# Chunked attention and a mixture of experts on one core: q and k loaded eight tokens to a partition, K read at strides

## The chip, the core and the metric

The kernel runs on one core of a Trainium2 chip. The core has five engines with instruction streams of their own: TensorE (PE in the profile, its weight loads PEld), VectorE (DVE), ScalarE (ACT), GpSimd (POOL) and SyncE (SP). PE multiplies matrices from the on-chip memory SBUF and writes the result to a second one, PSUM, from which DVE and ACT fetch it. DMA queues move data between the device's memory and SBUF. The metric is the device time of one execution in microseconds (us).

## The reference

```python
# attention: q, k, v are (4 batches, 8 heads, 768 tokens, 64)
chunk, left_ctx, right_ctx = (32, 16, 8)
for c in range(768 // 32):
    c_start, c_end = 32 * c, 32 * c + 32
    l_start, r_end = max(0, c_start - 16), min(768, c_end + 8)
    k_full = concatenate([mem_k, k[:, :, l_start:r_end]], axis=2)   # 8 + up to 56 keys
    v_full = concatenate([mem_v, v[:, :, l_start:r_end]], axis=2)
    a = softmax(q[:, :, c_start:c_end] @ k_full.T / 8)
    out[:, :, c_start:c_end] = a @ v_full
x = out.transpose(0, 2, 1, 3).reshape(3072, 512)      # tokens x all heads
# mixture of experts
y_dense = relu(x @ w1_dense) @ w2_dense
expert = argmax(x @ w_gate, axis=1)                   # one of 8 experts
gate = softmax(x @ w_gate)[token, expert]
y = y_dense + gate * (relu(x @ w1[expert]) @ w2[expert])
```

All arrays are float32; the result has 3072 rows of 512.

## The kernel before

**Attention** goes over 16 pairs, each of two heads of one batch. The 128 partitions hold the two heads' 64 dimensions beside each other. The order of all instructions is written out by hand for every engine's queue, and each engine takes its own in that order.

`load_qk` (line 258) brings q and k of a pair from the device's memory with a cast to bf16, each into a tile in which a partition holds `U = 6` consecutive tokens of both heads: partition p holds tokens 6p to 6p + 5. POOL issues these loads, q's and k's four pairs ahead. `transpose_qk` (line 357) then turns them on PE: for each of the six places u and each head one transpose, 64 columns of weights by 128 moving columns, into a PSUM bank `tp`. The bank holds the tokens sorted by u first: column u * 128 + p is token 6p + u. The copies out of the bank put the tokens back in order, reading the bank at strides:

```python
srcv = tp[:, :S].rearrange("d (u p) -> d p u", u=U)
nc.scalar.copy(dT.rearrange("d (p u) -> d p u", u=U), srcv)      # q, line 374
lo = nc.vector.tensor_copy(dst[:D, 0], srcv[:D])                 # k, first head, line 378
hi = nc.scalar.copy(dst[D:, 1], srcv[D:])                        # k, second head, line 379
```

k's copy goes to one of two tiles `kbd`, where each head has its own 64 partitions and its own half of the columns, with zeros elsewhere, so that one matmul gives both heads' scores.

`scores` (line 384) multiplies q with the memory keys (6 matmuls, line 388) and, for each of the 24 chunks, 32 query columns as weights with up to 56 key columns of both heads, 112 moving columns (line 401). The four chunks of a tile go to four column groups of PE. Then come `maximum` (DVE, line 411), `softmax` (subtraction on DVE, line 417, and the exponential on ACT, line 422), `probs_back` (PE transposes the probabilities, line 428, and ACT copies them out, line 430), `values` (line 438, in two halves of 12 chunks), and `scaled` (DVE, a reciprocal at line 449 and a product at line 450). `gate_part` and `gate_sum` work out the gate's logits: transposes at line 470, copies on ACT at line 473, matmuls at line 495, sums on DVE at lines 506 and 508. `record` casts the pair's result to bf16 into a row buffer (ACT, line 480) and puts each row's token number beside it (lines 485 and 487), from a small table `tok`: row p of tile t is token 128 t + p. `tok` is made once by an iota on POOL and cast to float by DVE in `constants_cast` (line 761) in the third pair.

In turn i of the main loop (line 794) the engines get, in this order: the scores of pair i + 1, `scaled` of pair i - 1, the probabilities' transposes of pair i, the maximum and softmax of pair i + 1, the first half of the values of pair i, `transpose_qk` of pair i + 2, the second half of the values, and `record` and `gate_sum` of pair i - 1. On DVE the copy of k thus stands between the softmax of pair i + 1 and `scaled` of pair i. On ACT the exponential, the copy of q and the copy of k follow one another.

**Routing.** When a batch is done, `choose`, `ranks` and `rank` find each token's expert and its row among that expert's rows (PE and DVE), and `rows_out` (line 585) scatters the rows into `x_reg` in the device's memory (POOL, line 589). Every row carries its gate and its token number.

**Experts.** `x_reg` is fetched in tiles of 128 rows (SP), transposed (line 204), multiplied with the dense weights (lines 218 and 234) and with the tile's expert's weights (lines 218 and 955), and the rows are scattered to the output by their token numbers (POOL, line 964).

Of the kernel before, what the change touches and what calls it, by code (L numbers as in the profile page):

```python
# [11 lines left out]
F32 = mybir.dt.float32  # L12
BF16 = mybir.dt.bfloat16
AF = mybir.ActivationFunctionType
ALU = mybir.AluOpType
AX = mybir.AxisListType
I32 = mybir.dt.int32
# [3 lines left out]
def kernel(  # L21
# [14 lines left out]
    nc = tc.nc  # L36

    B, H, S, D = q.shape
# [6 lines left out]
    KEYS = n_mem + CTX  # L45
# [2 lines left out]
    NP = H // 2  # L48
    T = S // 128
    CPT = 128 // CHUNK  # L50
    U = 6
    PU = S // U
    PE_, DVE_ = mybir.EngineType.PE, mybir.EngineType.DVE
    ACT_, POOL_, SP_ = (
# [23 lines left out]
    r_pool = ctx.enter_context(tc.tile_pool(name="r_pool", bufs=1))  # L78
# [22 lines left out]
    def bank():  # L101
        return ps2.tile([128, 512], F32, tag="tp", name="tp")

    identity = singles.tile([128, 128], BF16, name="identity")
# [15 lines left out]
    to_cast = []  # L120
# [124 lines left out]
    st_ = [dict() for _ in range(NPAIR)]  # L245
# [7 lines left out]
    NK = 2  # L253
    kbd = [a_const.tile([128, 2, S], BF16, name=f"kbd{i}") for i in range(NK)]
# [3 lines left out]
    def load_qk(pi, names="qk"):  # L258

        b, hp = divmod(pi, NP)  # L260
        for nm, src in (("q", q), ("k", k)):
            if nm not in names:
                continue
            t_ = a_load.tile([PU, 2, U * D], BF16, tag=f"{nm}_bf", name=f"{nm}_bf")
            nc.gpsimd.dma_start(
                t_, src[b, 2 * hp:2 * hp + 2].rearrange("h (p u) d -> p h (u d)", u=U)
            )
# [89 lines left out]
    def transpose_qk(pi):  # L357

        for nm in ("q", "k"):
            bf = st_[pi].pop(nm + "b")  # L360
            tp = bank().bitcast(BF16)
            for u in range(U):
                for hh in range(2):
                    r0 = hh * D
                    nc.tensor.transpose(  # L365
                        tp[r0:r0 + D, u * PU:(u + 1) * PU],
                        bf[:, hh, u * D:(u + 1) * D],
                        identity,
                        tile_position=(0, r0),
                    )  # L370
            srcv = tp[:, :S].rearrange("d (u p) -> d p u", u=U)
            if nm == "q":
                dT = a_work.tile([128, S], BF16, tag="qT", name="qT")
                nc.scalar.copy(dT.rearrange("d (p u) -> d p u", u=U), srcv)
                st_[pi]["qT"] = dT
            else:
                dst = kbd[pi % NK].rearrange("d h (p u) -> d h p u", u=U)
                lo = nc.vector.tensor_copy(dst[:D, 0], srcv[:D])  # L378
                hi = nc.scalar.copy(dst[D:, 1], srcv[D:])  # L379
                tc.declare_no_dep(  # L380
                    hi.ins, lo.ins, reason="the two heads have partitions of their own"
                )

    def scores(pi):
        qT, kb = st_[pi].pop("qT"), kbd[pi % NK]
        for t in range(T):
            o = (t % TB) * 2 * KEYS
            nc.tensor.matmul(
                sc[:, t // TB, o:o + 2 * KEYS].rearrange(
                    "p (h k) -> p h k", k=KEYS)[:, :, CTX:],  # L390
                qT[:, t * 128:(t + 1) * 128],
                mkT[:, pi],
            )
        for t in range(T):
            o = (t % TB) * 2 * KEYS
            for cc in range(CPT):
                c = t * CPT + cc
                l = max(0, c * CHUNK - LEFT)
                r = min(S, c * CHUNK + CHUNK + RIGHT)
                k0 = l - (c * CHUNK - LEFT)  # L400
                nc.tensor.matmul(  # L401
                    sc[cc * CHUNK:(cc + 1) * CHUNK, t // TB, o:o + 2 * KEYS].rearrange(
                        "p (h k) -> p h k", k=KEYS)[:, :, k0:k0 + r - l],
                    qT[:, c * CHUNK:(c + 1) * CHUNK],
                    kb[:, :, l:r],
                    tile_position=(0, cc * CHUNK),
                )

# [337 lines left out]
    def constants():  # L746
        nc.gpsimd.affine_select(
            upper, ones, pattern=[[1, 128]], compare_op=ALU.is_ge, fill=0.0,
            base=-1, channel_multiplier=-1,
        )  # L750
        slot_no = iota_f32(NB, "slot_no")
        slot128 = iota_f32(NB, "slot128", step=128)
        desc = iota_f32(E, "desc", base=E, step=-1)
        pcol = iota_f32(1, "pcol", step=0, cm=1)
        tok = iota_f32(T, "tok", step=128, cm=1)
        base_a = iota_f32(NA, "base_a", base=128, step=128)
        reg25 = iota_f32(E, "reg25", base=1, step=ROWS // 128)
        reg0 = iota_f32(E, "reg0", base=128, step=ROWS)
        return slot_no, slot128, desc, pcol, tok, base_a, reg25, reg0

    def constants_cast():
        for tf, ti in to_cast:
            nc.vector.tensor_copy(tf, ti)
        nc.vector.tensor_copy(seen_bf, reg25)

    transpose_qk(0)
    scores(0)
    maximum(0)
    softmax(0)
# [24 lines left out]
    for i in range(NPAIR):  # L794
# [69 lines left out]
        if i == 1:  # L864
            slot_no, slot128, desc, pcol, tok, base_a, reg25, reg0 = constants()
# [108 lines left out]
    while w_todo:  # L974
        src, dst = w_todo.pop(0)
# [82 lines left out]
```

## Time and profile before

| | |
|---|---|
| time, median of 3 runs | 240.48 us (240.46 to 241.56) |
| the profiled execution | 243.27 us |
| its span, first to last instruction | 241.5 us |
| mean granted TensorE clock | 0.966 |
| instructions | 7851 |
| PE busy | 198.7 us |
| DVE busy | 157.4 us |
| ACT busy | 135.5 us |
| POOL busy | 144.8 us |

The profile is of one execution. Its busy times say how long an engine had an instruction under way; how long a stage takes is decided by what its instructions wait for. In the rows that follow, `<-` after the busy time names what an engine was idle for. `x24` is a count of instructions; where a row merges several, its time runs from the first start to the last end.

### The profile page before, as it was taken

The page shows a single profiled execution, that of the slowest core. Times are in us where ns is not written, and L with a number is a line of the kernel's source. Part 1 is how long each engine was busy: PE and PEld are TensorE (multiplying, and loading weights), DVE is VectorE, ACT ScalarE, POOL GpSimd, SP SyncE. Part 2 cuts the span into 40 slices and gives each one's busy share as a digit, 9 for nine tenths or more (in the row PEclk, how much of TensorE's full clock was granted, in tenths as well). Part 3 has the DMA queues.
Part 4 walks back from the last instruction along what each step waited for, and adds up shares of the span by engine and source line. Part 5 has one row for each costly group of instructions (what it writes and reads, how often), then busy time and mean ns, then how long its engine had stood idle before and what let it go on. Part 6 is the DMA issues. An engine that isn't in the chain of part 4 may idle for free.

```text
span 241.5 us, 7851 instructions
## 1 busy us (share of the span) xinstructions
PE 198.7 (82%) x3147; PEld 148.4 (61%) x3147; DVE 157.4 (65%) x372; ACT 135.5 (56%) x205; POOL 144.8 (60%) x215
## 2 busy tenths in 40 slices
PE   1687597989788978887738999999999999999960
PEld 0466475766656656665517777777777866766630
DVE  4688969789878879878714661322224678788750
ACT  7257666896879777987322455555556622222210
POOL 7976983606997499958401871121222068888881
PEclk9999979999999999999795999999999999999997
DMA  5999999998999999999998549999999323433432
GB/s 89 195 178 159 131 164 182 167 155 152 147 177 188 161 146 178 200 167 250 192 174 166 104 101 184 264 189 201 184 148 174 62 90 155 182 129 123 164 138 83
DMA packets 59879, 38.57 MB, mean 160 GB/s; under 512 B 35646, under 2 KB 57534, under 8 KB 59840
## 3 DMA queue, kind: packets, MB, share of 16 engines
q0 software_dynamic: 21584, 25.20, 59.6%
q1 hardware_dynamic: 37216, 11.77, 29.1%
q10 hardware_dynamic: 1040, 1.06, 1.8%
q8 instruction: 27, 0.44, 0.8%
q14 instruction: 12, 0.10, 0.2%
HBM read 43.22 MB, written 11.30 MB: 226 GB/s over the span
## 4 chain that ended last, share of the span: by engine, by line
POOL 23%; DMA 20%; issue 10%; PE 6%; DVE 5%; ACT 2%; POOLq 1%; ACTq 0%; DVEq 0%
DMA w_all<-in_moe_w_dram 16%; POOL out_dram L964 12%; POOL x_reg L589 5%; POOL idle L583 4%; DMA x_reg<-rec,row_i 3%; PE sc L218 2%; PE av L438 1%; DVE x L450 1%; DMA xg<-x_reg 1%; PE tp L365 1%; DVE dif L417 1%; DVE mx L411 1%; ACT kbd L379 1%; PE tp L470 1%; POOLq L964 0%
## 5 line engine op out<-in xcount | busy, mean ns | idle before, releaser
L589 POOL DMA_INDIRECT x_reg<-rec,row_i x24 | 26.8, 1118 | 23.3 <-ACT rec L480 14.4
L964 POOL DMA_INDIRECT out_dram<-y,dst_i x27 | 29.0, 1074 | 14.3 <-DVE y L960 10.6
L438 PE MATMUL av<-vw,at 128*32 128x130 f32 x768 | 31.0, 296 | 7.0 <-issue 3.9
L438 PEld LDWEIGHTS av<-vw,at 128*32 128x32 f32 x768 | 22.1, 116 | 14.2 <-issue 8.7
L224 ACT ACTIVATE h<-sc 128x512 bf16<-128x512 f32 x27 | 16.1, 597 | 24.3 <-PE sc L218 24.3
L353 POOL COPY vw<-vw 24x1536 f32<-24x1536 f32 x15 | 23.2, 1545 | 10.6 <-DMA vw<-in_v_dram 6.5
L218 PEld LDWEIGHTS <-w_st 128*128 128x128 bf16 x432 | 25.5, 98 | 5.8 <-DVE w_st L942 3.2
L218 PEld LDWEIGHTS <-w1d 128*128 128x128 bf16 x432 | 27.0, 101 | 2.3 <-issue 1.8
L942 DVE COPY w_st<-w_all 128x2048 bf16 x27 | 19.8, 738 | 5.6 <-PE sc L218 4.1
L224 ACT ACTIVATE xT_B<-sc 128x512 bf16<-128x512 f32 x16 | 9.6, 597 | 23.4 <-PE sc L218 23.4
L378 DVE COPY kbd<-tp 64x768 bf16<-64x768 bf16 x16 | 15.2, 948 | 11.0 <-PE tp L365 11.0
L207 DVE COPY xT_B<-tp 128x512 bf16<-128x512 bf16 x16 | 6.8, 424 | 23.4 <-PE tp L204 23.3
L422 ACT ACTIVATE a<-dif 128x768 f32<-128x768 f32 x16 | 13.5, 844 | 13.9 <-DVE dif L417 12.2
L234 PE MATMUL av<-w2d,h 128*128 128x512 bf16 x72 | 19.2, 390 | 0.0
L977 POOL CAST scratch<-w_all 1x1 f32<-1x1 bf16 x10 | 1.7, 174 | 28.9 <-DMA w_all<-in_moe_w_dram 28.9
L473 ACT COPY xT<-tp 128x384 f32<-128x384 f32 x32 | 14.0, 489 | 6.8 <-PE tp L470 6.8
L470 PE MATMUL tp<-identity_f,x 128*128 128x128 f32 x96 | 13.6, 276 | 4.9 <-DVE x L450 2.4
L430 ACT COPY at<-at_ps 128x768 f32<-128x768 f32 x16 | 12.8, 798 | 7.8 <-PE at_ps L428 7.6
L218 PE MATMUL sc<-xT_B,w_st 128*128 128x128 bf16 x256 | 16.9, 219 | 0.2 <-DVE w_st L942 0.2
L218 PE MATMUL sc<-xT_B,w1d 128*128 128x128 bf16 x256 | 16.9, 219 | 0.0
L411 DVE TENSOR_REDUCE mx<-sc 128x12 f32<-128x768 f32 x16 | 15.3, 956 | 1.7 <-PE sc L401 1.3
L417 DVE TENSOR_TENSOR dif<-sc,mx 128x768 f32<-128x768 f32 x16 | 15.3, 958 | 1.6
(160 smaller groups left out, 449.2 us busy)
## 6 DMA issues: line engine op xcount, KB each, us to landing
w_all<-in_moe_w_dram POOLq DMA_DIRECT2D x14, 512.0 KB, 6.9
vw<-in_v_dram SPq DMA_DIRECT2D x30, 200.0 KB
xg<-x_reg SPq DMA_DIRECT2D x27, 129.0 KB
q_bf<-in_q_dram POOLq DMA_DIRECT2D x16, 192.0 KB, 7.7
k_bf<-in_k_dram POOLq DMA_DIRECT2D x16, 192.0 KB, 7.2
vw<-in_mem_v_dram SPq DMA_DIRECT2D x32, 48.0 KB
x_reg<-fill ACTq DMA_DIRECT2D x1, 1032.0 KB
w_all<-in_moe_w_dram POOLq DMA_DIRECT2D x4, 256.0 KB, 8.5
```

The costliest lines, as they stand in the source:

```text
L218: written(place, nc.tensor.matmul(ph[:, f, :], w[:, d, f * 128:(f + 1) * 128], xT[:, d, :], start=(d == 0), stop=(d == DT - 1),))
L224: was_read(place, nc.scalar.activation(h_sb, ph, AF.Relu))
L234: written(place, nc.tensor.matmul(pd, h_d[:, f, :], w2d_sb[:, f, :], start=(f == 0), stop=(f == FT - 1)))
L353: copy(vt[p0 + CHUNK:p0 + CTX, :NCH, hh, :D], vt[p0:p0 + n, 1:, hh, :D])
L378: lo = nc.vector.tensor_copy(dst[:D, 0], srcv[:D])
L411: nc.vector.reduce_max(mx, scv, axis=AX.X)
L417: nc.vector.tensor_tensor(dif.rearrange("p (b t) (h k) -> p b (t h) k", b=2, h=2), scv, mx.to_broadcast([128, 2, T, KEYS]), ALU.subtract,)
L438: nc.tensor.matmul(av[cc * CHUNK:(cc + 1) * CHUNK, t // TB, (t % TB) * W2:(t % TB + 1) * W2], at[:, t, cc * CHUNK:(cc + 1) * CHUNK], vt[:, ...
L470: nc.tensor.transpose(xtt[:, t * 128:(t + 1) * 128], xb[:, t0 + t, :], identity_f32)
L589: inst = nc.gpsimd.indirect_dma_start(x_reg, bass.IndirectOffsetOnAxis(ap=row_i[:, t:t + 1], axis=0), rec[:, t, :], None,)
L942: nc.vector.tensor_copy(w_st[:, None], w1_all[:, bass.ds(e_dve.pop(s), 1), :, :])
L964: inst = nc.gpsimd.indirect_dma_start(out, bass.IndirectOffsetOnAxis(ap=dst_i[:, s:s + 1], axis=0), y, None, bounds_check=N_tokens - 1, oo ...
```

## The change

q and k are loaded with eight tokens to a partition, on 96 partitions in place of 128. Each has 16 transposes of 96 moving columns in place of 12 of 128.

For k the bank keeps the order that the transposes give, sorted by u first, and so does `kbd`: both copies read and write runs. `scores` picks the keys of a chunk, which begin and end at multiples of eight tokens, out of `kbd` with an access pattern of a step of 96 elements over u, and its result has the keys in token order.

For q the transposes write to the bank at steps: in every group of 16 columns, the two tokens that two neighbouring partitions hold at place u lie side by side, so column 16 g + 2 u + s holds token 16 g + 8 s + u. The copy reads and writes runs, and the queries stay in that order, in which every group of 16 is complete. So the rows of the attention's result are permuted within groups of 16, and the table of token numbers is changed to match by six small DVE instructions, once.

```diff
-    U = 6
+    U = 8
     PU = S // U
...
             tp = bank().bitcast(BF16)
+            pairs = tp[:, :S].rearrange("d (g u s) -> d u g s", u=U, s=2)
+            plain = tp[:, :S].rearrange("d (u g s) -> d u g s", u=U, s=2)
+            to = pairs if nm == "q" else plain
             for u in range(U):
                 for hh in range(2):
                     r0 = hh * D
                     nc.tensor.transpose(
-                        tp[r0:r0 + D, u * PU:(u + 1) * PU],
+                        to[r0:r0 + D, u],
                         bf[:, hh, u * D:(u + 1) * D],
-                        identity,
+                        identity[:PU, :PU],
                         tile_position=(0, r0),
                     )
-            srcv = tp[:, :S].rearrange("d (u p) -> d p u", u=U)
             if nm == "q":
                 dT = a_work.tile([128, S], BF16, tag="qT", name="qT")
-                nc.scalar.copy(dT.rearrange("d (p u) -> d p u", u=U), srcv)
+                nc.scalar.copy(dT, tp[:, :S])
                 st_[pi]["qT"] = dT
             else:
-                dst = kbd[pi % NK].rearrange("d h (p u) -> d h p u", u=U)
-                lo = nc.vector.tensor_copy(dst[:D, 0], srcv[:D])
-                hi = nc.scalar.copy(dst[D:, 1], srcv[D:])
+                dst = kbd[pi % NK]
+                lo = nc.vector.tensor_copy(dst[:D, 0], tp[:D, :S])
+                hi = nc.scalar.copy(dst[D:, 1], tp[D:, :S])
...
-        qT, kb = st_[pi].pop("qT"), kbd[pi % NK]
+        qT = st_[pi].pop("qT")
+        kb = kbd[pi % NK].rearrange("d h (u p) -> d h p u", u=U)
...
                     sc[cc * CHUNK:(cc + 1) * CHUNK, t // TB, o:o + 2 * KEYS].rearrange(
-                        "p (h k) -> p h k", k=KEYS)[:, :, k0:k0 + r - l],
+                        "p (h k) -> p h k", k=KEYS)[:, :, k0:k0 + r - l].rearrange(
+                        "p h (j u) -> p h j u", u=U),
                     qT[:, c * CHUNK:(c + 1) * CHUNK],
-                    kb[:, :, l:r],
+                    kb[:, :, l // U:r // U],
                     tile_position=(0, cc * CHUNK),
...
         nc.vector.tensor_copy(seen_bf, reg25)
+        ti = [i_ for f_, i_ in to_cast if f_ is tok][0]
+        odd_i = r_pool.tile([128, T], I32, name="odd_i")
+        nc.vector.tensor_scalar(odd_i, ti, 1, None, ALU.bitwise_and)
+        place_i = r_pool.tile([128, T], I32, name="place_i")
+        nc.vector.tensor_scalar(
+            place_i, ti, 2 * U - 1, 1, ALU.bitwise_and, ALU.logical_shift_right
+        )
+        odd = r_pool.tile([128, T], F32, name="odd")
+        nc.vector.tensor_copy(odd, odd_i)
+        place = r_pool.tile([128, T], F32, name="place")
+        nc.vector.tensor_copy(place, place_i)
+        nc.vector.scalar_tensor_tensor(
+            odd, odd, float(U - 1), place, op0=ALU.mult, op1=ALU.subtract
+        )
+        nc.vector.tensor_tensor(tok, tok, odd, ALU.add)
```

## The prediction

> **What bounds the kernel now.** I read the page's first two parts first, then the windows of the attention part pair by pair, then the timeline inside two pairs, and last the groups of the copies and matmuls that the change touches.
>
> ```profile
> span 241.5 us, 7851 instructions
> ...
> PE 198.7 (82%) x3147; PEld 148.4 (61%) x3147; DVE 157.4 (65%) x372; ACT 135.5 (56%) x205; POOL 144.8 (60%) x215
> ```
>
> No engine is busy throughout, so the stages must be looked at apart. The windows view, cut at the starts of VectorE's copy of k (line 378), gives 13 pairs; these are the first, the two that differ most in the later half and the last, with the sum over all 13.
>
> ```profile
> 18.11:24.29 6.18, 4.72 (x118) 3.85 (x121) 5.10 (x7) 4.53 (x8) 4.21 (x5) 1.00 1.36 159
> ...
> 79.04:86.78 7.74, 5.89 (x131) 4.30 (x133) 6.22 (x15) 5.06 (x9) 4.73 (x5) 1.00 1.24 158
> 86.78:92.21 5.43, 5.15 (x128) 4.12 (x130) 5.23 (x9) 3.92 (x7) 4.90 (x7) 1.00 1.08 181
> ...
> 98.32:105.14 6.82, 5.35 (x126) 4.19 (x128) 5.23 (x11) 6.65 (x11) 6.78 (x9) 1.00 1.15 179
> sum 87.03, PE 70.56 PEld 54.34 DVE 73.10 ACT 67.26 POOL 63.59; mean PE 5.43 PEld 4.18 DVE 5.62 ACT 5.17 POOL 4.89
> ```
>
> The columns are window, length, then busy time of PE, PEld, DVE, ACT and POOL, the granted clock, the DMA share and GB/s. A pair takes 87.03 / 13 = 6.69 us, while the fullest engine, DVE, works 5.62 of it. So a pair is a ring of engines that wait for one another, and what is saved on one of them counts only where its instruction is the last to arrive. Behind the attention part comes another regime:
>
> ```profile
> 126.00:184.00 58.00, 56.41 (x654) 42.73 (x655) 22.18 (x116) 31.02 (x54) 19.03 (x40) 0.94 0.94 172
> ```
>
> There PE works 56.41 of 58.00 us on the experts' tiles, which need every batch routed. The change touches none of that work. I therefore let each microsecond of the attention part pass to the end one for one.
>
> The timeline from one set of scores to the next shows the ring:
>
> ```profile
> 94.40 0.48 PE L401 MATMUL sc<-kbd,qT 128*32 128x80 bf16 x24 [0.51 <-ACT kbd L379]
> ...
> 94.80 0.88 PE L428 MATMUL at_ps<-identity_f,a 128*128 128x128 f32 x6
> ...
> 95.71 0.80 ACT L430 COPY at<-at_ps 128x768 f32<-128x768 f32 x1 [0.51 <-PE at_ps L428]
> ...
> 96.61 0.87 PE L438 MATMUL av<-vw,at 128*32 128x130 f32 x24 [0.28 <-issue]
> ...
> 97.42 0.53 PE L365 MATMUL tp<-identity,q_bf 128*64 128x128 bf16 x12
> ...
> 97.77 0.50 PE L365 MATMUL tp<-identity,k_bf 128*64 128x128 bf16 x12
> ...
> 98.27 0.78 ACT L374 COPY qT<-tp 128x768 bf16<-128x768 bf16 x1
> 98.32 0.95 DVE L378 COPY kbd<-tp 64x768 bf16<-64x768 bf16 x1 [0.51 <-PE tp L365]
> ...
> 99.07 0.79 ACT L379 COPY kbd<-tp 64x768 bf16<-64x768 bf16 x1
> ...
> 99.92 0.47 PE L401 MATMUL sc<-kbd,qT 128*32 128x80 bf16 x24 [0.17 <-ACT kbd L379]
> ```
>
> The scores wait for ScalarE's copy of k's second head (99.07 + 0.79 = 99.86), which stands behind the copy of q on ACT. VectorE's copy of the first head had ended at 98.32 + 0.95 = 99.27, 0.6 us earlier. This ring of PE and ACT closes in 99.92 - 94.40 = 5.52 us. DVE mostly waits for PE at its k copy; the waits view for 10 to 107 us says how much:
>
> ```profile
> DVE kbd L378 <- PE tp L365: 10.2, 11, 2.1
> ```
>
> These are total us, times and the longest. The 10.2 us in 11 of 16 pairs are the slack that a faster copy mostly adds to.
>
> **The change part by part. 1, the copies.**
>
> ```profile
> L378 DVE COPY kbd<-tp 64x768 bf16<-64x768 bf16 x16 | 15.2, 948 | 11.0 <-PE tp L365 11.0
> ...
> L430 ACT COPY at<-at_ps 128x768 f32<-128x768 f32 x16 | 12.8, 798 | 7.8 <-PE at_ps L428 7.6
> L379 ACT COPY kbd<-tp 64x768 bf16<-64x768 bf16 x16 | 12.7, 793 | 1.7 <-PE tp L365 1.4
> L374 ACT COPY qT<-tp 128x768 bf16<-128x768 bf16 x16 | 12.6, 787 | 2.8 <-PE tp L365 2.8
> ...
> L207 DVE COPY xT_B<-tp 128x512 bf16<-128x512 bf16 x16 | 6.8, 424 | 23.4 <-PE tp L204 23.3
> ...
> L209 DVE TENSOR_TENSOR dst_i<-xg,far 128x1 int32<-128x1 f32 x27 | 4.0, 148 | 0.0
> ```
>
> ACT's two copies read PSUM at strides today and take 787 and 793 ns; line 430, which reads the same 768 elements in a run, takes 798. ACT gains nothing from runs. DVE does: a run of 512 bf16 elements takes it 424 ns. Taking the whole 424 as proportional gives 636 ns for 768; with the 148 ns that one element a row costs (last row) as a fixed part it is 0.15 + 0.274 x 1.5 = 0.56 us. I take 0.56 (an estimate), so 948 - 560 = 0.39 us less, 16 x 0.39 = 6.2 us of DVE. What is late next is the second half of the values, which VectorE's next instruction (line 449) needs:
>
> ```profile
> 65.70 0.87 PE L438 MATMUL av<-vw,at 128*32 128x130 f32 x24
> 65.82 0.95 DVE L378 COPY kbd<-tp 64x768 bf16<-64x768 bf16 x1 [0.60 <-PE tp L365]
> ...
> 66.69 0.21 DVE L449 RECIPROCAL rs<-av 128x12 f32<-128x12 f32 x1
> ```
>
> PE delivers at 65.70 + 0.87 = 66.57 and the reciprocal starts at 66.69, so 0.12 us is all that the shorter copy frees there. In a pair with routing (three of 16) and in the one with the constants' casts, other DVE work stands between and I count 0.3. That gives 12 x 0.12 + 4 x 0.3 = 2.6 us. Not all of it lies on the ring of PE and ACT: I take -2.0, between nothing and -6.2.
>
> **2, the scores' reads.** The 24 chunk matmuls of a pair keep their columns and their output; the moving operand is now read 2 bytes at a time, 192 bytes apart (768 / 8 x 2). No row of the trace has such a read. The same 24 matmuls at half the granted clock, early in the run, took
>
> ```profile
> 15.06 0.75 PE L401 MATMUL sc<-kbd,qT 128*32 128x80 bf16 x24
> ```
>
> against 0.48 above: 0.27 us more where columns come half as fast. The lower bound is nothing: ACT's strided copies cost no more than its run did, and fewer columns than now cannot come. The upper one is the four column groups, which now stream side by side, taking turns. One column goes by in about (0.36 / 12) x 2 / 128 = 0.47 ns when two groups share it (first row below), so 24 x 112 x 0.47 = 1.26 us in place of 0.31 (second row), 0.95 more.
>
> ```profile
> 91.18 0.36 PEld L365 LDWEIGHTS <-q_bf 128*64 128x64 bf16 x12 [0.20 <-issue]
> ...
> 94.40 0.32 PEld L401 LDWEIGHTS <-qT 128*32 128x32 bf16 x23 [0.49 <-issue]
> ```
>
> I take half rate, 0.27, as a single stride seems likelier to cost each stream a tick than to make them queue. It lies on the ring in the 12 pairs where DVE waits for PE (11 in the waits row, one more before 10 us, as the group row of line 378 has 11.0 us): 12 x 0.27 = +3.2; bounds 0 and 16 x 0.95 = +15.2. [...]
>
> **3, the transposes.** 24 of 128 columns become 32 of 96: the same 3072 columns. Issued at the rate of today's columns they take the same 0.36 + 0.36; if each instruction had its 0.03 us whatever its length, 8 more would cost 0.24 us a pair. Two at a time in 0.06 us are 128 columns at the rate above, so columns set the pace: I take 0, bounds -0.6 us (0.04 a pair for a shorter tail) and 12 x 0.24 = +2.9. The 128 additional transposes, 256 PE instructions, also have to be fetched. Stalls that name no releaser exist:
>
> ```profile
> 85.88 0.52 PE L365 MATMUL tp<-identity,q_bf 128*64 128x128 bf16 x11 [1.45 <-issue]
> ```
>
> One such more or less is 1.45 us either way; I take 0.
>
> **4, q's writes.** q's transposes write words of two elements, 32 bytes apart. No row writes PSUM so; lower bound 0, upper bound each q transpose at half rate, 0.36 us a pair. I take 0, since a pair of 2-byte elements still fills one word.
>
> **5, the token numbers.** Six small DVE instructions come behind the casts of the third pair:
>
> ```profile
> 33.72 1.42 DVE L763 CAST slot_no<-slot_no_i 128x20 f32<-128x20 int32 x1
> ...
> 35.27 0.15 DVE L763 CAST tok<-tok_i 128x6 f32<-128x6 int32 x1
> ...
> 35.46 0.21 ACT L485 ACTIVATE rec<-tok 128x6 f32<-128x6 f32 x1 [0.72 <-DVE tok L763]
> ...
> 35.87 0.23 DVE L449 RECIPROCAL rs<-av 128x12 f32<-128x12 f32 x1
> ```
>
> ```profile
> L638 DVE TENSOR_SCALAR jump<-dA 128x8 f32<-128x8 f32 x1 | 0.4, 410 | 0.0
> ...
> L630 DVE TENSOR_SCALAR ni<-ni 128x8 int32<-128x8 int32 x1 | 0.2, 170 | 0.0
> ```
>
> Six by 170 ns are 1.0 us, by 410 at most 2.5. They stand straight ahead of the reciprocal, and ACT, which already waits 0.72 for the token numbers at line 485, waits for them too, with its copy for the next values behind it. I take +1.0, between +0.5 and +2.5.
>
> **6, the loads.** Each q or k load has 192 rows in place of 256 and the same bytes.
>
> ```profile
> DMA packets 59879, 38.57 MB, mean 160 GB/s; under 512 B 35646, under 2 KB 57534, under 8 KB 59840
> ...
> q_bf<-in_q_dram POOLq DMA_DIRECT2D x16, 192.0 KB, 7.7
> ```
>
> 32 x 64 = 2048 of 59879 packets go. A load lands 7.7 us after issue and is issued some four pairs, 27 us, ahead, so nothing waits for it: 0. With that cover gone its gain would at most be a quarter of 7.7, 1.9 us once, at the start.
>
> Sum: -2.0 + 3.2 + 0 + 0 + 1.0 + 0 = +2.2. The profiled execution took 243.27 us (span 241.5 and 1.8 around it), 1.2% over the median of 240.48; 243.27 + 2.2 = 245.5, which on the median is 242.7.
>
> **The rivals.** B, on the other side: the strided read is free. Then scores cost as before, the copy's 2.6 us count in full and the shorter tail gives 0.6: -2.6 - 0.6 + 1.0 = -2.2, 238.3 us. For it: PE's ring then has nothing new. Against it: no row has such a read, and the copy's saving is capped by the values. It decides once the scores cost under 0.08 us a pair more (12 x 0.08 = 1.0, which leaves -1.2). C: the four column groups take turns, 12 x 0.95 = 11.4, with -2.0 + 1.0 gives +10.4, 250.9 us; scores would then take about 1.4 us. Against it: contiguous, all four stream at once today. D: q's scattered words halve PE's writes, 12 x 0.36 = 4.3 above the forecast, 247.0 us. ACT's 787 ns shows only that reading at strides is free, not writing. [...]
>
> **How the numbers follow.** The forecast A has 0.46 (its own range 240.8 to 245.0), B 0.28, C 0.12, D 0.14. Half a per cent, 1.2 us, is about what a measurement of this kernel can tell from no change: 239.3 to 241.7. Faster takes 0.24 of B and 0.03 of A, same 0.04 of B and 0.10 of A, the rest is slower: 0.27, 0.14, 0.59. The range 237.4 to 248.5 holds A, D and nearly all of B, and leaves C out.
>
> **What would show it.** Right: the copy of line 378's place near 560 ns and more DVE waiting for PE ahead of it; a pair's 24 scores near 0.75 us at full clock; q's transposes, like k's, within 0.4 us. Scores at 0.48 speak for B, at 1.2 or more for C; q's transposes far slower than k's for D. The prediction is wrong if the DVE copy was the ring's last arrival more often than the 5 pairs without a wait, or if fetch stalls move by several microseconds.

## The result and the profile after

The changed kernel took 250.25 us (median of 4 runs, 249.42 to 255.22) beside 241.02 us for the kernel before (240.46 to 242.33): a ratio of 1.036, with a 95% interval of 1.030 to 1.043. It is slower by some 9 us. The forecast was 242.7 us with a range up to 248.5; the sign was right, the size was not. Here and below a time is the median of all runs of a kernel, while a ratio compares only the fast ones among them, as every kernel has some executions that are some per cent slower.

The profiled execution of the changed kernel took 249.95 us. Its page, first part (busy time, share of the span, instructions by engine):

```profile
span 248.2 us, 8095 instructions
...
PE 208.5 (84%) x3257; PEld 157.2 (63%) x3275; DVE 152.4 (61%) x378; ACT 135.0 (54%) x205; POOL 142.2 (57%) x215
```

DVE works 5.0 us less than before (157.4), PE 9.8 us more (198.7). The groups of instructions by line, different shapes apart, tell which (the first number behind the bar is the busy time in us, the second the mean ns of one):

```profile
L404 PE MATMUL sc<-kbd,qT 128*32 128x112 bf16 x352 | 22.1, 373 | 2.9 <-issue 2.9
L415 DVE TENSOR_REDUCE mx<-sc 128x12 f32<-128x768 f32 x16 | 15.3, 956 | 7.9 <-PE sc L404 7.5
...
L381 ACT COPY kbd<-tp 64x768 bf16<-64x768 bf16 x16 | 12.7, 793 | 1.8 <-PE tp L368 1.4
L376 ACT COPY qT<-tp 128x768 bf16<-128x768 bf16 x16 | 12.6, 790 | 1.9 <-PE tp L368 1.8
...
L380 DVE COPY kbd<-tp 64x768 bf16<-64x768 bf16 x16 | 8.8, 548 | 11.4 <-PE tp L368 11.3
```

VectorE's copy of k fell from 948 to 548 ns; ScalarE's two copies stayed at 790 and 793. The scores are what grew. How much, the windows view of line 404 alone (line 401 before) says for the whole attention part. First the kernel after, then before (columns: window, length, then busy time of PE and PEld, granted clock, DMA share and GB/s):

```profile
8.00:125.00 117.00, 22.12 (x384) 14.28 (x384) 0.97 1.06 165
```

```profile
8.00:125.00 117.00, 8.16 (x384) 6.18 (x384) 0.97 1.18 172
```

The same 384 matmuls keep PE busy for 22.12 in place of 8.16 us: 13.96 more, or 0.87 in each of the 16 pairs. The granted clock is 0.97 in both. The timeline of the same pair that the prediction showed, after the change:

```profile
92.32 0.40 PEld L368 LDWEIGHTS <-q_bf 96*64 96x64 bf16 x16 [0.20 <-issue]
...
92.65 0.41 PEld L368 LDWEIGHTS <-k_bf 96*64 96x64 bf16 x16
...
93.24 0.55 DVE L380 COPY kbd<-tp 64x768 bf16<-64x768 bf16 x1 [0.34 <-PE tp L368]
...
94.16 0.79 ACT L381 COPY kbd<-tp 64x768 bf16<-64x768 bf16 x1
...
95.01 1.37 PE L404 MATMUL sc<-kbd,qT 128*32 128x80 bf16 x24 [0.34 <-ACT kbd L381]
...
96.31 0.88 PE L432 MATMUL at_ps<-identity_f,a 128*128 128x128 f32 x6
96.42 0.96 DVE L415 TENSOR_REDUCE mx<-sc 128x12 f32<-128x768 f32 x1 [0.15 <-PE sc L404]
...
97.22 0.80 ACT L434 COPY at<-at_ps 128x768 f32<-128x768 f32 x1 [1.41 <-PE at_ps L432]
```

The scores of a pair take 1.37 us where they took 0.48, and three things hang on them: the maximum (line 415) on VectorE, the next transposes of probabilities on PE (line 432), and through these ScalarE's copy of the probabilities (line 434), which now waits 1.41 us there (0.51 before). The waits view of 10 to 128 us shows it (total us, times, the longest), after and then before:

```profile
ACT at L434 <- PE at_ps L432: 24.6, 11, 5.3
...
DVE kbd L380 <- PE tp L368: 10.4, 12, 1.7
...
DVE mx L415 <- PE sc L404: 7.5, 6, 2.8
```

```profile
DVE kbd L378 <- PE tp L365: 10.2, 11, 2.1
...
ACT at L430 <- PE at_ps L428: 7.6, 11, 1.4
...
DVE mx L411 <- PE sc L401: 1.3, 2, 0.9
```

Both engines that come behind the scores wait for PE: ACT 17.0 us more at this line, the maximum 6.2 us more. Not all of that is new waiting. ScalarE's wait at line 473, 6.8 us before, is gone after the change; over all its lines in this stretch it waits 34.9 us in place of 30.2, and VectorE 26.4 in place of 19.9. The 13 pairs between VectorE's copies of k, first and last, and their sum:

```profile
19.11:26.48 7.37, 5.29 (x121) 4.13 (x114) 4.60 (x7) 4.90 (x8) 4.48 (x5) 1.00 1.04 150
...
106.03:113.32 7.29, 6.20 (x134) 4.81 (x137) 4.92 (x11) 6.52 (x10) 5.72 (x8) 1.00 1.21 173
sum 94.21, PE 80.74 PEld 62.24 DVE 69.62 ACT 66.46 POOL 61.44; mean PE 6.21 PEld 4.79 DVE 5.36 ACT 5.11 POOL 4.73
```

These took 87.03 us before and take 94.21. VectorE was the fullest engine with 5.62 us of a pair and now works 5.36; PE went from 5.43 to 6.21 and is the fullest. The last copy of k starts at 113.32 in place of 105.14, 8.2 us later. The profiled execution of the kernel before took 243.27 us, more than its median of 241.02. In the kernel *before_cast* below, which is as fast as the kernel before (ratio 1.002) and was profiled at 241.73 us, the last copy starts at 104.1, 9.2 us ahead of the changed kernel's. So all of the lost time has been lost by then. In the chain that ended last, shares of the span by engine, PE has 24% (6% before):

```profile
POOL 25%; PE 24%; DMA 19%; issue 14%; DVE 8%; ACT 7%; POOLq 1%; SPq 0%; ACTq 0%; DVEq 0%
```

### The profile page after: what moved, and what is told of

It reads as the page before. It is cut to its first block, busy times and chain, and to the rows that moved or that the text cites. A ratio compares the mean times of both kernels' runs of the same rounds, so it can differ in the third digit from the quotient of the medians.

```text
span 248.2 us, 8095 instructions
## 1 busy us (share of the span) xinstructions
PE 208.5 (84%) x3257; PEld 157.2 (63%) x3275; DVE 152.4 (61%) x378; ACT 135.0 (54%) x205; POOL 142.2 (57%) x215
## 2 busy tenths in 40 slices
DMA packets 57832, 38.58 MB, mean 155 GB/s; under 512 B 35646, under 2 KB 55486, under 8 KB 57792
## 4 chain that ended last, share of the span: by engine, by line
POOL 25%; PE 24%; DMA 19%; issue 14%; DVE 8%; ACT 7%; POOLq 1%; SPq 0%; ACTq 0%; DVEq 0%
DMA w_all<-in_moe_w_dram 15%; POOL out_dram L983 12%; PE sc L404 7%; PE av L442 5%; POOL x_reg L593 4%; POOL idle L587 4%; PE at_ps L432 3%; POOL vw L353 3%; PE tp L368 3%; DVE dif L421 2%; DMA k_bf<-in_k_dram 2%; PE tp L474 2%; DMA xg<-x_reg 2%; DVE mx L415 2%; ACT kbd L381 2%
## 5 line engine op out<-in xcount | busy, mean ns | idle before, releaser
L442 PE MATMUL av<-vw,at 128*32 128x130 f32 x768 | 27.9, 279 | 4.4 <-issue 3.5
L353 POOL COPY vw<-vw 24x1536 f32<-24x1536 f32 x15 | 22.6, 1509 | 12.4 <-DMA vw<-in_v_dram 8.7
L404 PE MATMUL sc<-kbd,qT 128*32 128x112 bf16 (+2 forms) x384 | 22.1, 369 | 7.5 <-issue 2.9
L442 PEld LDWEIGHTS av<-vw,at 128*32 128x32 f32 x768 | 20.3, 111 | 10.3 <-issue 5.4
L404 PEld LDWEIGHTS <-qT 128*32 128x32 bf16 x384 | 14.3, 110 | 9.1 <-issue 4.7
L234 PE MATMUL av<-w2d,h 128*128 128x512 bf16 x66 | 18.2, 388 | 0.5 <-issue 0.2
L432 PE MATMUL at_ps<-identity_f,a 128*128 128x128 f32 x96 | 15.8, 308 | 1.6 <-ACT a L426 1.6
```

Of the source, the lines that this page charges most:

```text
L234: written(place, nc.tensor.matmul(pd, h_d[:, f, :], w2d_sb[:, f, :], start=(f == 0), stop=(f == FT - 1)))
L353: copy(vt[p0 + CHUNK:p0 + CTX, :NCH, hh, :D], vt[p0:p0 + n, 1:, hh, :D])
L404: nc.tensor.matmul(sc[cc * CHUNK:(cc + 1) * CHUNK, t // TB, o:o + 2 * KEYS].rearrange("p (h k) -> p h k", k=KEYS)[:, :, k0:k0 + r - l].rea ...
L432: nc.tensor.transpose(at_ps[:, t, :], a_sb[:, t, :], identity_f32)
L442: nc.tensor.matmul(av[cc * CHUNK:(cc + 1) * CHUNK, t // TB, (t % TB) * W2:(t % TB + 1) * W2], at[:, t, cc * CHUNK:(cc + 1) * CHUNK], vt[:, ...
```

## The experiments

**Which part costs.** The theory after the result: the read at strides alone makes the loss. The rivals: the eight tokens to a partition (more transposes, other loads), q's scattered writes, the table of token numbers. Four kernels take the parts one by one.

*run_read* is the changed kernel with one edit, a run in place of the step:

```diff
-        kb = kbd[pi % NK].rearrange("d h (u p) -> d h p u", u=U)
+        kb = kbd[pi % NK].rearrange("d h (j u) -> d h j u", u=U)
```

> The changed kernel with one thing different: the 24 score matmuls of a pair read their 56 keys as a run of neighbouring columns, through an access pattern with the same three loops. The keys are then taken in the bank's order, so the scores belong to other tokens; the amount of work is the same. Theory 1 (the strided read is the whole loss): a pair's 24 score matmuls go back from 1.35 to about 0.48 us and the time from 250.25 to 238.5 to 240.5 us, below the kernel before, as only the copy's gain and the token table's cost are left. Theory 2 (the read is part of it, and the permuted q, the table and 256 more PE instructions take the rest): the matmuls go back just the same, but the time stays at 243 to 247 us.

*k_alone* takes eight tokens and K at strides, but q as before, copied at strides into token order, and no table (the cut of its six instructions is not shown):

```diff
-            to = pairs if nm == "q" else plain
+            to = plain
...
-                nc.scalar.copy(dT, tp[:, :S])
+                nc.scalar.copy(dT.rearrange("d (p u) -> d p u", u=U),
+                               tp[:, :S].rearrange("d (u p) -> d p u", u=U))
```

> K's half of the change alone: eight tokens to a partition, k copied in runs and read at strides; q's transposes write in the plain order and its copy puts the tokens in order as before, so there is no new token table. Theory 1: as slow as the whole change, 248.5 to 251 us, less about 1.0 us for the table. Theory 2: 244 to 247 us.

*q_alone* takes eight tokens, q's pairs and the table, but k's copies put the keys in token order, which the scores read in a run with run_read's line:

```diff
-                dst = kbd[pi % NK]
-                lo = nc.vector.tensor_copy(dst[:D, 0], tp[:D, :S])
-                hi = nc.scalar.copy(dst[D:, 1], tp[D:, :S])
+                dst = kbd[pi % NK].rearrange("d h (p u) -> d h p u", u=U)
+                srcv = tp[:, :S].rearrange("d (u p) -> d p u", u=U)
+                lo = nc.vector.tensor_copy(dst[:D, 0], srcv[:D])
+                hi = nc.scalar.copy(dst[D:, 1], srcv[D:])
```

> Q's half alone: eight tokens to a partition, q's transposes write pairs, its copy goes in runs, the token table is changed; k is copied at strides into token order and read in runs as before. Theory 1: the kernel before plus the table's six small instructions, 240.5 to 242.5 us. Theory 2: 243 to 246 us.

*swap* is q_alone with the engines exchanged: VectorE copies q, which is a run, and ScalarE both heads of k at strides:

```diff
-                nc.scalar.copy(dT, tp[:, :S])
+                nc.vector.tensor_copy(dT, tp[:, :S])
...
-                lo = nc.vector.tensor_copy(dst[:D, 0], srcv[:D])
+                lo = nc.scalar.copy(dst[:D, 0], srcv[:D])
```

> A version meant to keep the gain without the strided read: q, whose bank is in the order in which it stays, is copied in a run by VectorE (about 0.55 us in place of 0.95 for k's first head); both heads of k are copied by ScalarE at strides into token order, which costs that engine the same 0.79 us each as q and k's second head did; the scores read runs. Theory 1: scores 0.48 us a pair, and the ring of PE and ACT as before, so 238.5 to 241 us: the kernel before less 1 to 2.6 us for VectorE plus 1.0 us for the table. Theory 2: 243 us or more, as in q's half alone.

| kernel | median us (before 241.69) | ratio to before, 95% interval | scores of a pair, us |
|---|---|---|---|
| run_read | 241.48 | 1.001 (0.996 to 1.007) | 0.47 to 0.48 |
| k_alone | 249.3 | no interval (four runs, 245.04 to 252.48) | 1.35 |
| q_alone | 244.69 | 1.011 (1.003 to 1.019) | 0.47 to 0.48 |
| swap | 242.58 | 1.005 (1.000 to 1.010) | 0.47 to 0.48 |

The timeline of run_read, the answer to the pair above:

```profile
91.95 0.48 PE L404 MATMUL sc<-kbd,qT 128*32 128x80 bf16 x24 [0.51 <-ACT kbd L381]
...
93.27 0.80 ACT L434 COPY at<-at_ps 128x768 f32<-128x768 f32 x1 [0.51 <-PE at_ps L432]
```

With one line changed the scores are back at 0.48 us and ScalarE's wait at 0.51. The time is that of the kernel before within 0.7%: 1.036 less 1.001 leaves 0.035 of 241 us, 8.5 us, for the read at strides, which is the whole loss. The other parts together come to nothing that can be measured; a gain of one may hide a cost of another, and the 238.5 to 240.5 us expected from the shorter copy did not come. The scores of run_read belong to other tokens and send the rows to other experts, but the experts' part has 27 tiles in it as in the kernel before. k_alone shows the slow scores without q's part or the table; its four runs spread too far for a ratio. swap has no read at strides on PE and is not faster than before either: nothing was gained by handing ScalarE the strides.

**What about the read is slow.** The step is 192 bytes here. Is it the distance, and do the four column groups take turns at the memory (the mechanism of rival C), or is each of them slowed by itself? *step4*, *step8* and *step16* read keys 4, 8 and 16 bytes apart, with as many columns in as many matmuls (of other keys than the reference's); *one_group* keeps 192 bytes and sends all 24 matmuls to the same column group, so three quarters of the scores are not written.

```diff
-        kb = kbd[pi % NK].rearrange("d h (u p) -> d h p u", u=U)
+        kb = kbd[pi % NK]
...
-                    kb[:, :, l // U:r // U],
+                    kb[:, :, min(l, S - 56 * 2):][:, :, :(r - l) * 2].rearrange(
+                        "d h (j u x) -> d h x j u", u=U, x=2)[:, :, 0],
```

This is step4; step8 has 4 in place of 2, step16 takes the same distance from a nest as in the changed kernel:

```diff
+                    kb[:, :, min(l, S - 8 * 8):][:, :, :8 * 8].rearrange(
+                        "d h (u p) -> d h p u", p=8)[:, :, :(r - l) // U],
```

> The changed kernel with the keys of a chunk read 4 bytes apart (every second column) in place of 192; other keys are taken than the reference's, the work is the same. What is looked at is the time of a pair's 24 score matmuls. Theory A (what counts is whether neighbouring reads fall into one 16-byte piece): 0.48 us at full clock, as in a run. Theory B (any step costs): 1.35 us.

> The same with 8 bytes between the keys. Theory A: two reads to a piece, 0.48 us, at most 0.75. Theory B: 1.35 us. A cost that grows with the step: between the two, some 0.7 to 0.9 us.

> The same with 16 bytes between the keys inside a group of eight. Theory A: every read in another piece, so the full 1.35 us as with 192 bytes. A cost that grows with the step: about 1.0 us. Theory B: 1.35 us.

one_group:

```diff
-                    sc[cc * CHUNK:(cc + 1) * CHUNK, t // TB, o:o + 2 * KEYS].rearrange(
+                    sc[:CHUNK, t // TB, o:o + 2 * KEYS].rearrange(
...
-                    tile_position=(0, cc * CHUNK),
+                    tile_position=(0, 0),
```

> The changed kernel, read at 192 bytes, with all 24 score matmuls of a pair sent to the first column group of PE in place of four in turn; three quarters of the scores are then not written, which leaves their softmax over other values and moves tokens to other experts, so only the scores' own time is read. Theory C (the four streams take turns at one supply of elements, 24 x 112 in 0.91 us, 0.34 ns each): one stream alone gets all of it and is held by its columns, 24 x 47 ns, so 1.1 to 1.5 us, no slower than now. Theory D (each stream is slowed by itself to 1.4 to 1.9 ns an element, and the four run side by side): 24 x 150 to 210 ns, 3.6 to 5.0 us.

The timelines, one set of scores each, of step4, step8, step16 and one_group:

```profile
87.97 0.49 PE L404 MATMUL sc<-kbd,qT 128*32 128x80 bf16 x24 [0.51 <-ACT kbd L381]
```

```profile
91.28 0.78 PE L404 MATMUL sc<-kbd,qT 128*32 128x80 bf16 x24 [0.51 <-ACT kbd L381]
```

```profile
91.79 1.33 PE L404 MATMUL sc<-kbd,qT 128*32 128x80 bf16 x24
```

```profile
83.64 4.64 PE L404 MATMUL sc<-kbd,qT 128*32 128x80 bf16 x24
```

| step between keys | 2 B (run_read) | 4 B | 8 B | 16 B | 192 B (after) |
|---|---|---|---|---|---|
| scores of a pair, us | 0.48 | 0.49 | 0.78 | 1.33 | 1.37 |
| time of one run, us (before, beside these, 245.55) | – | 242.93 | 245.56 | 251.54 | – |

Two bytes more cost next to nothing (0.49 against 0.48 us), 8 bytes make the scores 1.6 times as long, 16 bytes 2.8 times, and from there to 192 bytes 0.04 us comes on top. So it is not the distance as such; what fits these five times is how many keys lie in the same 16 bytes: 8, 4, 2, 1, 1. With two keys there (8 bytes apart) the scores took 0.78 us, so two were not enough to be free, and four were. Why the rise ends there, no run shows.

one_group: if the four column groups took turns at the memory, putting them in one would change nothing, about 1.37 us. It took 4.64 us, 3.4 times as long (328.08 us for the run). So the four streams do run side by side, and each is slowed by itself. The 24 matmuls have 22 x 112 + 80 + 96 = 2640 columns; one stream alone takes 4.64 us / 2640 = 1.76 ns for a column. A quarter of the columns at that rate is 1.16 us (an estimate), of the 1.37 that four groups take together. The sets of one_group that start before 120 us took 4.64 or 4.65 us each, the one at 83.64 at a granted clock of 0.83 (83.64 to 88.20 us), the one at 11.29 beside transposes that take 0.85 us in place of 0.53: neither shows in the time of a set.

**A read in pairs.** Since 4 bytes between the keys cost next to nothing (0.49 against 0.48 us), k's transposes could write pairs as q's do. *pairs_k* does this; a chunk's keys then take two matmuls in place of one of 112 columns: of its seven groups of eight keys four are read with s = 0 (64 columns) and three with s = 1 (48).

```diff
-            to = pairs if nm == "q" else plain
+            to = pairs
...
-        kb = kbd[pi % NK].rearrange("d h (u p) -> d h p u", u=U)
+        kb = kbd[pi % NK].rearrange("d h (g u s) -> d h s g u", u=U, s=2)
...
+                for s in range(2):
+                    g0, g1 = l // (2 * U), (r // U + 1 - s) // 2
...
-                    kb[:, :, l // U:r // U],
+                        kb[:, :, s, g0:g1],
```

> The whole change with k's transposes writing pairs like q's, so that the keys of a half group lie 4 bytes apart, a step that cost nothing when it was tried; as the half groups of 8 no longer follow one another evenly, a chunk needs two score matmuls of 64 and 48 columns in place of one of 112. The copies go in runs as in the change. Expected: 48 matmuls in 0.65 to 0.8 us a pair in place of 1.35, and 241.5 to 244.5 us, near q's half alone; if the 384 additional matmuls and weight loads cost more than their columns, 246 us or more.

*best* is pairs_k with both heads of k copied by VectorE (twice 0.55 us) and the constants' casts ahead of `transpose_qk`:

```diff
-                hi = nc.scalar.copy(dst[D:, 1], tp[D:, :S])
+                hi = nc.vector.tensor_copy(dst[D:, 1], tp[D:, :S])
...
+        if i == 2:
+            constants_cast()
         if i + 2 < NPAIR:
             transpose_qk(i + 2)
-        if i == 2:
-            constants_cast()
```

> The same with VectorE copying both heads of k, 0.55 us each, so that ScalarE's ring loses 0.79 us a pair, and with the casts and the token table moved ahead of the third pair's copy of k. If the ring of PE and ACT sets the pair, 0.2 to 0.4 us less a pair, 237 to 240.5 us, ahead of both kernels. If DVE takes over, which then has 0.15 us more a pair than in the kernel before, no better than the kernel before: 240.5 to 243 us.

pairs_k took 254.15 us beside 243.11 before, ratio 1.056 (1.044 to 1.067), best 256.93 us, 1.067 (1.056 to 1.078). Both are slower than the changed kernel, though their scores are quick. The timeline of pairs_k on PE:

```profile
64.86 0.58 PE L406 MATMUL sc<-kbd,qT 128*32 128x48 bf16 x48 [0.51 <-ACT kbd L381]
70.28 0.34 PE L406 MATMUL sc<-kbd,qT 128*32 128x48 bf16 x20
73.75 0.55 PE L406 MATMUL sc<-kbd,qT 128*32 128x64 bf16 x28 [3.12 <-issue]
74.22 1.54 PE L435 MATMUL at_ps<-identity_f,a 128*128 128x128 f32 x6
```

and its windows right before and behind that wait:

```profile
70.00:73.70 3.70, 0.63 (x29) 0.47 (x27) 1.95 (x2) 1.06 (x2) 3.34 (x5) 1.00 1.05 162
73.70:77.00 3.30, 3.25 (x44) 2.86 (x43) 2.28 (x3) 1.18 (x2) 3.09 (x5) 0.51 1.18 136
```

An undisturbed pair of scores takes 0.58 us, so pairs 4 bytes apart are quick even in 48 matmuls. But in the midst of a set PE stands still for 3.12 us, with no releaser, and works at a granted clock of 0.51 behind it: the probabilities' transposes (line 435) take 1.54 us, where line 432 took 0.88. The scores wait like this five times; PE's waits put down to issue on matmuls between 10 and 128 us:

```profile
PE sc L406 <- issue: 9.7, 5, 3.1
PE av L445 <- issue: 6.8, 10, 2.7
...
PE tp L368 <- issue: 1.5, 1, 1.5
```

18.0 us in all, 6.8 in the changed kernel: 11.2 us more. Against that stand the 0.79 us a pair that the scores are quicker (1.37 less 0.58), 12.6 us if all 16 pairs passed it on. pairs_k has 768 instructions more (8863 against 8095). The queue that carries instructions, in the DMA view of before, after and pairs_k (packets, MB, share of 16 engines):

```profile
q8 instruction: 27, 0.44, 0.8%
```

```profile
q8 instruction: 28, 0.46, 0.8%
```

```profile
q8 instruction: 31, 0.51, 0.9%
```

The 244 instructions that the change adds come with one packet more, pairs_k's next 768 with three: about one for every 256.

Whether PE's stops are waits for such packets, the traces tell, as they hold the time of every packet and of every instruction. Number PE's instructions by their start, weight loads and its sequencer's own among them. In pairs_k PE stands still for more than 0.9 us seven times between 40 and 128 us, and goes on with the instructions 1730, 1986, 2754, 3010, 4034, 4290 and 4802. All of these lie a multiple of 256 apart. A packet of the instruction queue ends 0.98 to 1.74 us ahead of each: the stop of 3.12 us ends at 73.75, a packet at 72.28. In the kernel before and the changed one the stops at places of the same row (706, 2242, 2754 and 706, 962, 1218) end 1.40 to 1.80 us behind a packet. By these places and times PE waits there for its next 256 instructions. Two of these stops name another releaser in the waits view: VectorE's line 454 (2.3 us in the changed kernel) and ScalarE's line 353 (3.0 us in pairs_k). Counted at these places, between 10 and 130 us, PE's stops behind a packet are 4.6 us before, 5.6 after the change and 19.0 in pairs_k. The 13.4 us by which pairs_k exceeds the changed kernel are more than the 12.6 that its scores are quicker. Why three packets more bring so many more stops, no run shows.

**Eight tokens alone, and the casts.** q_alone at 1.011 left a doubt whether eight tokens cost something by themselves. *u8_only* is q_alone with q copied at strides too, and without the table: only `U = 8` remains. *before_cast* is the kernel before with the constants' casts ahead of `transpose_qk`, the move that best makes.

```diff
-            to = pairs if nm == "q" else plain
+            to = plain
...
-                nc.scalar.copy(dT, tp[:, :S])
+                nc.scalar.copy(dT.rearrange("d (p u) -> d p u", u=U), srcv)
```

> Eight tokens to a partition and nothing else: 16 transposes of 96 columns in place of 12 of 128, loads on 96 partitions, both tensors copied at strides into token order and read in runs, no new token table. Theory 3 (what q's half cost beyond the kernel before is the token table, six DVE instructions ahead of what DVE and ACT wait for): like the kernel before, 0.995 to 1.004 of it. Theory 4 (it is the 256 additional PE instructions or the loads): as slow as q's half, 1.006 to 1.015.

> The kernel before with the constants' casts one step earlier in VectorE's order: ahead of its copy of k in the third pair, where it waited 2.1 us for PE, in place of behind it, where the reciprocal and ScalarE waited for them. If DVE's place in that pair decides, 1 to 2 us less (ratio 0.992 to 0.996); if the pair is set by PE's own stalls, no change (0.998 to 1.002).

u8_only: 245.08 us beside 243.11, ratio 1.016 (1.006 to 1.027). before_cast: 241.05 us, 1.002 (0.993 to 1.010), no difference. So nothing says that the table is what q_alone paid for. Eight tokens bring 256 more PE instructions and loads with other rows. *more_tr* adds the instructions alone to the kernel before, *fewer_tr* keeps the loads of eight tokens and takes the instructions away.

```diff
-            for u in range(U):
+            for u in [0, 1] + list(range(U)):
```

> The kernel before (six tokens to a partition, its loads, copies and reads), but of each pair's transposes of q and of k the first four of each are issued twice, so 128 transposes with their weight loads, 256 PE instructions, come on top, as many as eight tokens to a partition bring; the values stay the same. Theory I (the number of PE instructions, which have to be fetched, is what eight tokens to a partition cost): ratio 1.010 to 1.02 to the kernel before, PE's waits named issue between 10 and 128 us above the 7.6 us of the kernel before. Theory L (the loads with rows of eight tokens on 96 partitions cost it): ratio 1.000 within 0.004. Theory T (columns: the extra transposes stream 128 columns each, 8 a pair, 0.24 us a pair): 16 x 0.24 = 3.8 us at most, so at most 1.016, and the transposes of a pair take 0.47 and 0.47 in place of 0.36 and 0.36; this one would not follow for eight tokens, whose columns are the same in sum.

```diff
-            for u in range(U):
+            for u in range(4, U):
+                nc.tensor.transpose(
+                    to[:, u],
+                    bf[:, u % 2, u // 2 * 2 * D:(u // 2 + 1) * 2 * D],
+                    identity[:PU, :PU],
+                )
+            for u in range(4):
```

> The kernel u8_only (eight tokens to a partition, both copies at strides, no table), but half of each pair's transposes take two tokens of one head at once, 128 columns, so that q and k need 12 transposes each as with six tokens; the heads of these tokens come out in the wrong rows, so the scores are computed from mixed heads. Loads and copies as with eight tokens, PE instructions as many as in the kernel before. Theory I: ratio 1.000 within 0.004, and PE's waits named issue near 7.6 us. Theory L: ratio 1.010 to 1.02 as in u8_only. If both kernels of this call lie at 1.000, the two only cost together or the 1.016 of u8_only lay in its few runs.

They gave 252.53 and 251.61 us beside 250.21 for the kernel before, whose own runs spread from 241.88 to 253.84 us there, so nothing can be read from it. The same kernels again, under the names *more_tr2*, *fewer_tr2* and, for u8_only, *u8_again*, side by side:

> The kernel of more_tr again, since the runs of the kernel before spread from 241.9 to 253.8 us there and no ratio can be read from them. Theory I (the number of PE instructions): ratio 1.010 to 1.02. Theory L (the loads): 1.000 within 0.004. Of the chain in the attention part, the last scores would start later by the transposes' 16 x 0.24 = 3.8 us at most.

> The kernel of fewer_tr again, for the same reason. Theory I: 1.000 within 0.004. Theory L: 1.010 to 1.02.

> The kernel u8_only once more, so that it shares the runs of the kernel before with the other two. If what it cost (1.016, interval 1.006 to 1.027) is real, 1.008 to 1.02; if it was an accident of its six runs, within 0.004 of 1.000, and then neither the loads nor the instructions have anything to explain.

| kernel | median us (before 242.15) | ratio to before, 95% interval |
|---|---|---|
| more_tr2 (instructions without the loads) | 244.42 | 1.011 (1.003 to 1.019) |
| fewer_tr2 (loads without the instructions) | 242.82 | 1.008 (1.004 to 1.013) |
| u8_again (both) | 243.18 | 1.003 (0.998 to 1.009) |

Both halves show about 1%, and the two together less than either. more_tr2 also has a third more columns of transposes, which eight tokens don't have (q's take PE 11.5 us in place of 9.6), so its 1.1% may come from them. The intervals overlap, and u8_again does not repeat the 1.016 of u8_only. Eight tokens alone cost between nothing and some 1.6%; which of the two it would be stays open.

## Why the prediction was right or wrong

**The ring of PE and ACT** held. What PE does more in the scores came to the end: of 13.96 us of busy time, 8.2 to 9.2 us at the last copy of k and 8.5 us by run_read, so as many as 10 of the 16 pairs (8.5 / 0.87) pass it on; the interval of the two ratios together, about 2 us to each side, makes that 7 to 12. The prediction had 12.

**Term 2, the scores' reads, is the step that failed.** It took 0.27 us a pair ("half rate"); measured is 0.87. The mechanism, a step of 2-byte reads that slows each stream, was right, its size was a third of the real one. With 0.87 the prediction's own sum is -2.0 + 12 x 0.87 + 1.0 = +9.4 us, or 250.4 us on the 241.02 of the kernel before, against the 250.25 measured. That this is so close is partly luck: 12 pairs for some 10, and -1.0 us for the other terms where run_read shows +0.3, offset each other. The reason for choosing 0.27 was weak. It came from the slow scores early in the run, read as half the granted clock; the window over that row says otherwise:

```profile
15.06:15.81 0.75, 0.75 (x27) 0.50 (x24) 0.25 (x2) 0.75 (x1) 0.75 (x1) 1.00 1.55 152
```

The granted clock is 1.00 there. PE is slow in these first microseconds, where it reads runs, for a reason that the profile doesn't name. The changed kernel shows it in the same stretch:

```profile
9.77 1.36 PE L404 MATMUL sc<-kbd,qT 128*32 128x80 bf16 x24 [0.63 <-ACT kbd L381]
11.06 0.85 PE L368 MATMUL tp<-identity,q_bf 96*64 96x96 bf16 x16
```

The transposes take 0.85 there and 0.53 later, the scores at strides 1.36 as everywhere else. The upper bound of 0.95 a pair did hold the value, yet was set aside as the less likely mechanism.

**Rival C** gave 250.9 us and scores of 1.4 us, both right as numbers, for a wrong reason: it had the column groups take turns, and one_group excludes that. A measured time that fits a rival's number isn't proof of its mechanism.

**Rival B** falls: the read isn't free, a pair's scores take 1.37 us in place of 0.48.

**Term 1, the copies.** VectorE's copy came to 548 ns for an estimate of 560, and ScalarE's gained nothing, as foreseen (787 to 790, 793 to 793 ns). VectorE's wait at it grew only from 10.2 to 10.4 us, so the sign that the prediction named, more waiting there, did not show; VectorE now waits elsewhere, at the maximum. What the shorter copy brings to the end, taken at -2.0, was not measured apart: run_read holds it together with the table and the eight tokens, at 0.3 us slower than before with an interval from 1.0 faster to 1.6 slower. The prediction's terms without the read, -2.0 + 1.0 = -1.0, lie at its edge.

**Term 3, the transposes.** 16 of 96 columns take 0.40 and 0.41 us of weight loads in a pair, 12 of 128 took 0.36. That is the small increase that lay within the bounds (0.24 a pair for both). Fetch stalls are the part taken at nothing. PE's waits put down to issue are 6.8 us in the changed kernel and 7.6 before (3.9 + 2.3 + 1.4, windows of 10 to 128 us); counted behind instruction packets, as above, the stops are 5.6 and 4.6 us. So they explain at most some 1 us of the loss. What eight tokens cost by themselves stays open, at 0 to 1.6%.

**Term 4 and rival D.** q's transposes, which write scattered pairs, take 0.40 us by their weight loads and 218 ns a matmul, k's, which write runs, 0.41 us and 216 ns. The scattered writes cost next to nothing here; D falls.

**Term 5, the table.** The six instructions, first and last, and the reciprocal behind them, in the timeline after:

```profile
37.77 0.16 DVE L771 TENSOR_SCALAR odd_i<-tok_i 128x6 int32<-128x6 int32 x1
...
38.45 0.17 DVE L783 TENSOR_TENSOR tok<-tok,odd 128x6 f32<-128x6 f32 x1
38.53 0.23 DVE L453 RECIPROCAL rs<-av 128x12 f32<-128x12 f32 x1
```

From the first start to the reciprocal are 0.76 us, near the 1.0 taken; what of it reaches the end, no run shows by itself.

**Term 6, the loads.** The packets fell by 2047 to 57832, for 2048 predicted, and q lands 7.4 us after issue (7.7): hidden, as foreseen.

## What to carry to other kernels

A layout that saves an engine a strided copy moves the stride to the reader, and the reader here is PE, which paid 0.87 us a pair more for the 0.40 that VectorE saved and stands on the ring; cost the read in time per column before trading for a copy that only adds slack. The scores of a pair took 0.48 us with bf16 keys 2 bytes apart and 0.49 with 4, but 0.78 with 8, 1.33 with 16 and 1.37 with 192. A number in the trace that stands in for an unseen cost needs the same cause as the cost: a slow phase of PE said nothing of strided reads.

## What was unexpected of the hardware

- A moving operand in bf16 read 192 bytes apart takes 1.76 ns a column in one stream (4.64 us for 2640 columns), one such set at a granted clock of 0.83. Four column groups side by side together need 1.37 us.
- The scores at strides take 1.36 us also where PE is slow for everything else (transposes 0.85 in place of 0.53 us, at 9.77 to 11.91 us), so the read sets their pace there, and not PE.
- PE's transposes that write 2 x 2 bytes every 32 bytes take 0.40 us for 16 by their weight loads, like those that write runs (0.41).
- PE's seven stops of over 0.9 us in pairs_k, between 40 and 128 us, all stand a multiple of 256 of its instructions apart, and end 0.98 to 1.74 us behind a packet of the instruction queue.
- With 768 more instructions, 9% of the program, PE stood still at the scores five times, up to 3.12 us, and worked at a granted clock of 0.51 behind such a stop; the kernel took 5.6% more than before, though its scores were nearly as quick.
